# A transformer block in one kernel: wo's low parts on POOL around z, kv's masking behind the denominators, other PSUM banks for the kv transposes, and one more set of q logits

## The chip, the cores and the metric

The kernel runs on one core of a Trainium2 chip. The metric is the device time of the whole kernel in microseconds; lower is better. The core's engines are TensorE (PE, matmuls; PEld is its weight load), VectorE (DVE), ScalarE (ACT), GpSimd (POOL) and SyncE (SP), which issues most DMAs. Each works through its own queue in order and waits on semaphores for what others produce.

## The reference

Sequence 2048, width 512, 32 heads of 16, hidden size 1792 of the token MLP, all float32. The block is a linear attention with learned softmax features, then an MLP over the token axis:

```python
pq = einsum("bhsd,hdf->bhsf", q, w_phi); pk = einsum("bhsd,hdf->bhsf", k, w_phi)
phi_q = concat([softmax(pq), softmax(-pq)], -1)
phi_k = concat([softmax(pk), softmax(-pk)], -1)
kv  = einsum("bhsf,bhsd->bhfd", phi_k, v)
z   = einsum("bhsf->bhf", phi_k)
num = einsum("bhqf,bhfd->bhqd", phi_q, kv)
den = einsum("bhqf,bhf->bhq", phi_q, z)[..., None] + 1e-6
h   = x + (num / den merged over heads) @ wo          # q, k, v = layernorm(x) @ wqkv
u   = gelu(einsum("bsd,sf->bdf", layernorm(h), w1) + b1)
out = h + transpose(einsum("bdf,fs->bds", u, w2) + b2)
```

## The kernel before

The tokens are cut into 16 tiles of 128 (`NT`). Float32 products are made from high and low parts in fp32r: `mm3` (lines 59 to 63) issues hi*hi, lo*hi or hi*lo, and the third, so a 128x512 product over four blocks of the width is twelve matmuls. `split` (line 54) makes the parts: ACT copies the high part, another engine subtracts it.

**First stage** (from line 330). For each tile t: project and exponentiate k (`k_logits`), project v (`v_proj`), add to kv in PSUM (`kv`, line 188, tile `kvp`), normalise phi_k (`k_norm`) and add it to `zacc`, from which z comes. For six tiles q is projected here too: `q_mm` (line 304) projects the next tile of q into one of two PSUM banks of the pool `ps_q`; `q_logits` (line 309) takes the maxima and minima per head on DVE, writes the shifted logits to an `eq` tile on DVE (line 138) and, from the seventh tile on, a plain copy on ACT (line 140, the last reader of the bank). `negate` (line 149) finishes that half on POOL; `q_exp` is an exp on ACT; `q_sums` sums on DVE.

**Transition** (lines 352 to 453). From line 353 on the order of PE, DVE, ACT and POOL is the order in which the code issues, by hand; SP's order is left to the scheduler. Here the last tiles of v and kv are made, wo is loaded into `WO` (line 370) and split into `woh` (`wo_hi`, ACT) and `wol` (`wo_lo`, DVE). z is a product of `zacc` with ones (line 426), copied to `zB` on ACT. `s_ez` (line 374, POOL) multiplies an exponentiated q tile by z, `s_den` (line 378, six operations on DVE) makes from it the factor `W`, `s_pq` (line 393, POOL) multiplies the q tile by `W`. At its end kv is masked into `kvS` (DVE, line 449), transposed on PE into a bank of the pool `ps_v` (line 452) and copied to `kvB` on ACT (line 453). When the pools of the first stage close (line 456), the banks of `ps_k`, `ps_v` and `ps_kv` are used again by `ps_f` (MLP sums), `ps_t` (transposes and numerators, tiles `tn`) and `ps_o` (output products, tile `po`).

**Loop** (line 557, counter `it`, 19 passes). Per pass PE does `s_num(it-1)` (32 small matmuls with `kvB`, line 481), `s_wo(it-2)` (twelve matmuls with woh and wol into `po`), `s_tr(it)` (eight transposes into `tn`), one `q_mm` (two in it=1), and from it=4 on `fill` for the first MLP product. `lead` (line 396) issues `s_pq(it+1)`, `s_ez(it+3)`, a `negate`, the `q_mm` and a `q_exp`. DVE then does `s_ol` (the low part of the numerators, tile `ol`; its high part `oh` is ACT's), the logits, two sums and a denominator interleaved, then `s_h` (adds `po` to the loaded x as tile `h`, statistics), then the low parts of streamed weights (`wlo`). The one `tn` buffer is read by `oh` and `ol` before the next transposes, the one `po` buffer by `h` before the next `s_wo`. `FN[p]` and `FL[p]` count how far the fills and weight loads of F-pair p have come; the second pair starts (line 582) when all sixteen q logits are made.

After the loop come the rest of the first MLP product with its gelu (line 641) and the second product (line 689), both mostly PE.

Of the kernel before, what the change touches and what calls it, by code (L numbers as in the profile page):

```python
# [9 lines left out]
F32 = mybir.dt.float32  # L10
F32R = mybir.dt.float32r
AF = mybir.ActivationFunctionType
# [5 lines left out]
P = 128  # L18
S, D, H, DH, F = 2048, 512, 32, 16, 1792
NT = S // P  # L20
KD = D // P
# [12 lines left out]
def block_kernel(ctx: ExitStack, tc: tile.TileContext, x, xT, wT, phibd, wo, w1, b1, w2, b2,  # L34
                 kvmask, ident_in, out):
    nc = tc.nc
# [4 lines left out]
    ident = cst.tile([P, P], F32, name="ident")  # L41
# [28 lines left out]
    wqp = aq.enter_context(tc.tile_pool(name="wqp", bufs=1, side="right"))  # L70
    wqh = wqp.tile([P, KD, D], F32R, name="wqh")
    wql = wqp.tile([P, KD, D], F32R, name="wql")
    kvB = wqp.tile([P, 2, P], F32, name="kvB")
    wqp.tile([P, 504], F32, name="pad")
    wk = aq.enter_context(tc.tile_pool(name="wk", bufs=4, side="right"))

# [6 lines left out]
    wp = a1.enter_context(tc.tile_pool(name="wp", bufs=1))  # L83
# [1 line left out]
    wvh = wp.tile([P, KD, D], F32R, name="wvh")  # L85
    wvl = wp.tile([P, KD, D], F32R, name="wvl")
    zacc = wp.tile([P, NG, P], F32, name="zacc")
    kvS = wp.tile([P, 4, 64], F32, name="kvS")
    ps_k = a1.enter_context(tc.tile_pool(name="ps_k", bufs=2, space=PSUM))
    ps_v = a1.enter_context(tc.tile_pool(name="ps_v", bufs=2, space=PSUM))  # L90
    ps_kv = a1.enter_context(tc.tile_pool(name="ps_kv", bufs=1, space=PSUM))
# [26 lines left out]
    def proj(t, wh, wl, pool, name):  # L118
        o = pool.tile([P, D], F32, name=name, tag=name)
        for kt in range(KD):  # L120
            mm3(o, X[t][:, 0, kt, :], X[t][:, 1, kt, :], wh[:, kt, :], wl[:, kt, :],
                kt == 0, kt == KD - 1)
        return o
# [6 lines left out]
    def logit_ops(src, e, pool):  # L130

        v = src.rearrange("p (j h d) -> p j h d", h=2, d=DH)
        ev = signs(e)
        mx = wk.tile([P, NPR, 2], F32, name="mx")
        mn = wk.tile([P, NPR, 2], F32, name="mn")

        def shift():
            nc.vector.tensor_sub(ev[:, :, 0], v, mx.unsqueeze(3).to_broadcast([P, NPR, 2, DH]))
            if pool:
                nc.scalar.activation(ev[:, :, 1], v, AF.Copy)  # L140
                MN.append((ev, mn))
            else:
                nc.vector.tensor_sub(ev[:, :, 1], mn.unsqueeze(3).to_broadcast([P, NPR, 2, DH]), v)

        return [lambda: nc.vector.tensor_reduce(mx, v, axis=AX.X, op=ALU.max),
                lambda: nc.vector.tensor_reduce(mn, v, axis=AX.X, op=ALU.min),
                shift]
# [7 lines left out]
    def run(*lists):  # L155

        for i in range(max(map(len, lists))):
            for ops in lists:
                if i < len(ops):
                    ops[i]()  # L160

    def exps(t, e):
        nc.scalar.activation(e, e, AF.Exp, scale=r1[:, t:t + 1])

    def heads(e):
        return e.rearrange("p g (a d) -> p (g a) d", d=DH)
# [11 lines left out]
    def k_norm(t, z=True):  # L178
        sk = wk.tile([P, 2 * H], F32, name="sk", bufs=2)
        nc.vector.reduce_sum(sk, heads(PK[t]), axis=AX.X)  # L180
        nc.vector.reciprocal(sk, sk)
        nc.gpsimd.tensor_mul(heads(PK[t]), heads(PK[t]), sk.unsqueeze(2).to_broadcast([P, 2 * H, DH]))  # L182
        if z and t == 0:
            nc.gpsimd.tensor_copy(zacc, PK[t])
        elif z:
            nc.gpsimd.tensor_add(zacc, zacc, PK[t])  # L186

    def kv(t):

        for n in range(4):  # L190
            for c in range(4):
                g = n // 2 * 4 + c
                j = 2 * g + n % 2
                nc.tensor.matmul(kvp[32 * c:32 * c + 32, n, :], VS[t][:, 32 * j:32 * j + 32],
                                 PK[t][:, g, n % 2 * 64:n % 2 * 64 + 64], start=(t == 0 and n == 0),
                                 stop=(t == NT - 1), skip_group_check=True)
# [107 lines left out]
    def q_mm():  # L304
        if q["mm"] < NT:
            PS[q["mm"]] = proj(q["mm"], wqh, wql, ps_q, "pu")
            q["mm"] += 1

    def q_logits(lag):
        n = q["logits"]  # L310
        if n < min(NT, q["mm"] - lag + NT * (q["mm"] == NT)):
            EQ[n] = big.tile([P, NG, P], F32, name="eq", tag="big")
            q["logits"] += 1
            return logit_ops(PS[n], EQ[n], n >= len(Q_AT))
        return []

    def q_exp(lag):
        n = q["exp"]
        if n < min(NT, q["logits"] - len(MN) - lag):
            exps(n, EQ[n])  # L320
            q["exp"] += 1

    def q_sums(lag):
        n = q["sum"]
        if n < min(NT, q["exp"] - lag + NT * (q["exp"] == NT)):
            q["sum"] += 1
            return q_sum(n)
        return []
# [29 lines left out]
    woh = w2p.tile([P, KD, D], F32R, name="woh")  # L358
    wol = w2p.tile([P, KD, D], F32R, name="wol")

    def wo_hi(j):
        nc.scalar.activation(woh[:, j], WO[j], AF.Copy)

    def wo_lo(j):
        nc.vector.tensor_sub(wol[:, j], WO[j], woh[:, j])

    WO = {}
    for j in range(KD):
# [5 lines left out]
    def s_ez(t):  # L374
        EZ[t] = az.tile([P, NG, P], F32, name="ez")
        nc.gpsimd.tensor_mul(EZ[t], EQ[t], zB)  # L376
# [16 lines left out]
    def s_pq(t):  # L393
        nc.gpsimd.tensor_mul(heads(EQ[t]), heads(EQ[t]), W[t].rearrange("p g c h -> p (g c h)").unsqueeze(2).to_broadcast([P, 2 * H, DH]))  # L394

    def lead(it, mm):

        if 0 <= it + 1 < NT:
            s_pq(it + 1)
        if 0 <= it + 3 < NT:  # L400
            s_ez(it + 3)
        negate()
        for _ in range(mm):
            q_mm()
        q_exp(0)

    def v_kv():
        nonlocal v
        v_proj(v)
        kv(v - 1)  # L410
        v += 1
# [3 lines left out]
    nc.gpsimd.tensor_add(zacc, zacc, PK[NT - 2])  # L415
    q_mm()
    k_norm(NT - 1, False)
    v_kv()
    run(q_logits(0))
    nc.vector.tensor_add(zacc, zacc, PK[NT - 1])  # L420
    negate()
    q_exp(0)
    zB = big.tile([P, NG, P], F32, name="zB", tag="big")
    for g in range(2):
        pz = ps_k.tile([P, 4, P], F32, name="pk_ps")
        nc.tensor.matmul(pz, ones, zacc[:, 4 * g:4 * g + 4, :], start=True, stop=True)
        nc.scalar.activation(zB[:, 4 * g:4 * g + 4, :], pz, AF.Copy)  # L427
    s_ez(0)
    s_ez(1)
    q_mm()  # L430
    v_kv()
    run(s_den(0))
    run(q_logits(0))
    for j in range(KD):
        wo_hi(j)
    s_pq(0)
    negate()
    q_exp(0)
# [2 lines left out]
    v_kv()  # L441
    run(s_den(1))
    run(q_logits(0))
    for j in range(KD):
        wo_lo(j)
    assert v == NT
    kv(NT - 1)
    q_mm()
    nc.vector.tensor_mul(kvS, kvp, mask.unsqueeze(1).to_broadcast([P, 4, 64]))
    pt = ps_v.tile([P, 2, P], F32, name="pv")  # L450
    for b in range(2):
        nc.tensor.transpose(pt[:, b, :], kvS[:, 2 * b:2 * b + 2, :].rearrange("p n f -> p (n f)"), ident)
    nc.scalar.activation(kvB, pt, AF.Copy)


    a1.close()
# [6 lines left out]
    ps_o = a2.enter_context(tc.tile_pool(name="ps_o", bufs=1, space=PSUM, reuse_waits="tile"))  # L463
    HN, HT, PHT, OS, PO, VE = {}, {}, {}, {}, {}, {}

    def s_tr(t):
        PHT[t] = ak.tile([P, NG, P], F32, name="pht")
        ptr = ps_t.tile([P, 2, 4, P], F32, name="tn")
        for g in range(NG):
            nc.tensor.transpose(ptr[:, g // 4, g % 4, :], EQ[t][:, g, :], ident)  # L470
        for half in range(2):
            nc.scalar.activation(PHT[t][:, half * 4:half * 4 + 4, :], ptr[:, half], AF.Copy)  # L472

    def s_num(t):

# [12 lines left out]
    def s_ol(t):  # L488
        oh, ol, pn = OS[t]
        return [lambda: nc.vector.tensor_sub(ol, pn, oh)]  # L490
# [66 lines left out]
    for it in range(NT + 3):  # L557
        if 0 <= it < NT:
            s_x(it)
        if 0 <= it - 3 < NT:  # L560
            s_rstd(it - 3)
        if 0 <= it - 1 < NT:
            s_num(it - 1)
        if 0 <= it - 2 < NT:
            s_wo(it - 2)
        if it == 1:
            q_mm()
        if 0 <= it < NT:
            s_tr(it)
        lead(it, 1)  # L570
        den = s_den(it + 2) if it + 2 < NT else []
        run((s_ol(it - 1) if 0 <= it - 1 < NT else []) + q_logits(1) + (q_sums(0) if it > 0 else []), den)
        if it > 0:
            negate()
        if 0 <= it - 3 < NT:
            s_hn(it - 3)
        if 0 <= it - 2 < NT:
            s_h(it - 2)
        if FN[0] <= it - LAG:
            fill(0, ps_f)  # L580
        for _ in range(2):
            if q["logits"] == NT and FN[1] <= it - LAG:
                fill(1, ps_q)
        for p in range(2):
            if it >= LAG - 2 and FL[p] <= FN[p] + 1:
                fill_load(p)
# [198 lines left out]
```

## Time and profile before

| | |
|---|---|
| median of 3 runs | 568.13 us (567.6 to 568.39) |
| profiled execution | 566.03 us, of which 564.3 us span |
| mean granted PE clock | 0.986 |
| busy PE / PEld / DVE / ACT / POOL | 95% / 81% / 71% / 45% / 41% |
| longest groups on the chain that ended last | products into `py` (second MLP product) 25%, products into `pu` (q and first MLP product) 30% |

The page of the profile gives busy times per engine, the span in 40 slices, the DMA queues, the chain of work that ended last and the costliest groups of instructions. Other views give each engine's instructions in order of time with the idle time before them and what ended it, the waits of an engine summed by what it waited for, and the busy times in chosen stretches. In a row of the time view the first number is the start in us from the span's start, the second the duration (of several where "xN" stands), then engine, line, operation, and tiles written and read; in brackets the engine's idle time before it and its releaser. A row of a stretch gives its length, then the busy time of PE, PEld, DVE, ACT and POOL with counts, the granted clock, the DMA share and GB/s.

### The profile page before, as it was taken

Reading aid. Unit: us, or ns where it says so; the run is one execution under the profiler, and the core shown is the slowest. Engines: PE = TensorE matmul, PEld = TensorE weight load, DVE = VectorE, ACT = ScalarE, POOL = GpSimd, SP = SyncE. Lnnn points to the kernel's source line nnn. Section 1 sums busy time; section 2 is a strip of 40 time slices with the busy share of each in tenths; the row PEclk is TensorE's granted clock in tenths of the full one; section 3 lists DMA queues with packets and bytes.
Section 4 is the critical chain, followed back from the end, with each engine's and each line's share of the span. In section 5 each row is a group of like instructions: output and inputs, shape, how many; then the busy total and the mean of one; then the engine's idle time right before and its main releaser. Section 6 shows DMA issues by size and latency. Waiting matters only on the chain.

```text
span 564.3 us, 9893 instructions
## 1 busy us (share of the span) xinstructions
PE 535.8 (95%) x3872; PEld 456.4 (81%) x3872; DVE 401.3 (71%) x730; ACT 256.7 (45%) x402; POOL 229.4 (41%) x179
## 2 busy tenths in 40 slices
PE   7999999999778888999999999999999999999996
PEld 6787778777556666877778778888889999999996
DVE  4884999974975659999644893222765888878874
ACT  5599834423343336444454752332643333333330
POOL 1369799785834766889643220000000111101110
PEclk9999999999988979999999999999999999999999
DMA  8444301022200212333325544333102664456631
GB/s 290 129 113 131 113 20 57 1 58 95 75 1 20 76 56 53 117 113 114 123 88 175 153 143 127 105 98 93 57 20 74 150 150 105 131 140 150 150 68 45
DMA packets 52014, 56.06 MB, mean 99 GB/s; under 512 B 3840, under 2 KB 41600, under 8 KB 51968
## 3 DMA queue, kind: packets, MB, share of 16 engines
q1 hardware_dynamic: 49808, 51.64, 29.8%
q0 software_dynamic: 2016, 3.67, 4.7%
q8 instruction: 30, 0.49, 0.4%
q14 instruction: 16, 0.13, 0.1%
q10 hardware_dynamic: 144, 0.13, 0.1%
HBM read 47.04 MB, written 8.39 MB: 98 GB/s over the span
## 4 chain that ended last, share of the span: by engine, by line
PE 84%; DVE 6%; ACT 4%; DMA 2%; issue 1%; POOL 1%; SPq 0%; DVEq 0%; POOLq 0%; ACTq 0%
PE py L678 25%; PE pu L61 10%; PE pu L63 10%; PE pu L62 10%; PE po L61 3%; PE pk_ps L61 3%; PE pk_ps L62 3%; PE pk_ps L63 3%; PE tn L470 3%; PE po L62 2%; PE po L63 2%; PE pv L61 2%; PE pv L62 2%; PE pv L63 2%; PE tn L481 2%
## 5 line engine op out<-in xcount | busy, mean ns | idle before, releaser
L57 DVE TENSOR_TENSOR wlo<-wraw,whi 128x512 fp32r<-128x512 f32 (+1 forms) x84 | 99.8, 1199 | 69.5 <-ACT whi L56 69.3
L56 ACT ACTIVATE whi<-wraw 128x512 fp32r<-128x512 f32 (+1 forms) x84 | 81.9, 985 | 128.1 <-PE py L678 73.8
L678 PE MATMUL py<-uf,whi 128*128 128x256 f32 x560 | 96.2, 283 | 0.0
L716 POOL DMA_DIRECT2D out<-ot x14 | 12.5, 999 | 205.0 <-DVE ot L714 205.0
L61 PE MATMUL pu<-hs,whi 128*128 128x512 f32 x224 | 87.8, 395 | 0.6 <-ACT eq L140 0.6
L62 PE MATMUL pu<-hs,whi 128*128 128x512 f32 x224 | 87.4, 390 | 0.0
L63 PE MATMUL pu<-hs,wlo 128*128 128x512 f32 x224 | 86.3, 391 | 0.4 <-DVE wlo L57 0.4
L678 PEld LDWEIGHTS py<-uf,whi 128*128 128x128 f32 x560 | 83.3, 192 | 0.0
L678 PE MATMUL py<-uf,wlo 128*128 128x256 f32 x280 | 69.9, 283 | 0.0
L63 PEld LDWEIGHTS pu<-hs,wlo 128*128 128x128 f32 x224 | 42.0, 188 | 10.2 <-DVE wlo L57 1.5
L61 PEld LDWEIGHTS pu<-hs,whi 128*128 128x128 f32 x224 | 42.2, 189 | 9.4 <-ACT eq L140 1.1
L678 PEld LDWEIGHTS py<-uf,wlo 128*128 128x128 f32 x280 | 49.7, 192 | 0.0
L62 PEld LDWEIGHTS pu<-hs,whi 128*128 128x128 f32 x224 | 42.2, 189 | 8.5
L472 ACT ACTIVATE pht<-tn 128x512 f32<-128x512 f32 x32 | 17.4, 596 | 49.0 <-PE tn L470 49.0
L376 POOL TENSOR_TENSOR ez<-eq,zB 128x1024 f32<-128x1024 f32 x16 | 38.6, 2418 | 2.2 <-ACT zB L427 2.2
L61 PE MATMUL pu<-wqh,xs 128*128 128x512 f32 x64 | 28.8, 450 | 10.9 <-ACT eq L140 10.9
L678 PE MATMUL py<-un,whi 128*128 128x256 f32 x224 | 38.4, 283 | 0.0
L182 POOL TENSOR_TENSOR pk<-pk,sk 128x1024 f32<-128x1024 f32 x16 | 31.1, 1942 | 9.3 <-ACT xs L56 3.0
L394 POOL TENSOR_TENSOR eq<-eq,w 128x1024 f32<-128x1024 f32 x16 | 31.0, 1938 | 6.1 <-DVE w L391 6.1
L678 PEld LDWEIGHTS py<-un,whi 128*128 128x128 f32 x224 | 33.2, 192 | 0.1
L186 POOL TENSOR_TENSOR zacc<-zacc,pk 128x1024 f32<-128x1024 f32 x13 | 31.2, 2403 | 0.5
L57 POOL TENSOR_TENSOR xs<-xraw,xs 128x512 fp32r<-128x512 f32 x16 | 20.4, 1292 | 25.1 <-ACT xs L56 25.1
(152 smaller groups left out, 1161.0 us busy)
## 6 DMA issues: line engine op xcount, KB each, us to landing
wraw<-in_w SPq DMA_DIRECT2D x112, 256.0 KB, 2.9
xraw<-in_xT SPq DMA_DIRECT2D x16, 256.0 KB, 3.2
xh<-in_x SPq DMA_DIRECT2D x16, 256.0 KB, 2.6
h<-in_x SPq DMA_DIRECT2D x16, 256.0 KB, 2.9
out<-h SPq DMA_DIRECT2D x16, 256.0 KB, 2.5
out<-ot POOLq DMA_DIRECT2D x14, 256.0 KB, 4.3
wraw<-in_wT SPq DMA_DIRECT2D x12, 256.0 KB, 5.3
wo<-in_wo SPq DMA_DIRECT2D x4, 256.0 KB, 4.1
```

What stands on the lines that cost most here:

```text
L56: nc.scalar.activation(hi, src, AF.Copy)
L57: lo_engine.tensor_sub(lo, src, hi)
L61: nc.tensor.matmul(o, ah, bh, start=first, stop=False)
L62: nc.tensor.matmul(o, ah, bl, start=False, stop=False)
L63: nc.tensor.matmul(o, al, bh, start=False, stop=last)
L182: nc.gpsimd.tensor_mul(heads(PK[t]), heads(PK[t]), sk.unsqueeze(2).to_broadcast([P, 2 * H, DH]))
L186: nc.gpsimd.tensor_add(zacc, zacc, PK[t])
L376: nc.gpsimd.tensor_mul(EZ[t], EQ[t], zB)
L394: nc.gpsimd.tensor_mul(heads(EQ[t]), heads(EQ[t]), W[t].rearrange("p g c h -> p (g c h)").unsqueeze(2).to_broadcast([P, 2 * H, DH]))
L470: nc.tensor.transpose(ptr[:, g // 4, g % 4, :], EQ[t][:, g, :], ident)
L472: nc.scalar.activation(PHT[t][:, half * 4:half * 4 + 4, :], ptr[:, half], AF.Copy)
L678: nc.tensor.matmul(o, a[x], b[:, y], start=start and i == 0, stop=stop and i == 2, skip_group_check=True)
```

## The change

The edit touches the transition and the first pass of the loop.

- `wo_lo` subtracts on POOL instead of DVE. All four `wo_hi` and the first two `wo_lo` are issued after `k_norm` of the last tile; the other two `wo_lo` after the first two `s_ez`.
- The first `q_exp` of the transition is issued after z's copies instead of before them.
- The last `q_mm` of the transition is issued ahead of `kv(NT - 1)` instead of behind it.
- `kvS` moves to another pool; its mask stays behind the second denominator and logits, no longer behind the four `wo_lo`. Its transposes and the copy to `kvB` become `s_kv`, issued in it=0 after `s_tr(0)`, with a PSUM tile of `ps_o` instead of `ps_v`.
- In it=0 one more `q_logits` is issued, so that eleven sets of logits are made by its end instead of ten.

```diff
@@ wqp (stays to the loop's end) / wp (first stage only)
     kvB = wqp.tile([P, 2, P], F32, name="kvB")
+    kvS = wqp.tile([P, 4, 64], F32, name="kvS")
...
-    kvS = wp.tile([P, 4, 64], F32, name="kvS")
...
     def wo_lo(j):
-        nc.vector.tensor_sub(wol[:, j], WO[j], woh[:, j])
+        nc.gpsimd.tensor_sub(wol[:, j], WO[j], woh[:, j])
...
     k_norm(NT - 1, False)
+    for j in range(KD):
+        wo_hi(j)
+    wo_lo(0)
+    wo_lo(1)
     v_kv()
     run(q_logits(0))
     nc.vector.tensor_add(zacc, zacc, PK[NT - 1])
     negate()
-    q_exp(0)
     zB = big.tile([P, NG, P], F32, name="zB", tag="big")
...
         nc.scalar.activation(zB[:, 4 * g:4 * g + 4, :], pz, AF.Copy)
+    q_exp(0)
     s_ez(0)
     s_ez(1)
+    wo_lo(2)
+    wo_lo(3)
     q_mm()
     v_kv()
     run(s_den(0))
     run(q_logits(0))
-    for j in range(KD):
-        wo_hi(j)
     s_pq(0)
...
     run(q_logits(0))
-    for j in range(KD):
-        wo_lo(j)
     assert v == NT
+    q_mm()
     kv(NT - 1)
-    q_mm()
     nc.vector.tensor_mul(kvS, kvp, mask.unsqueeze(1).to_broadcast([P, 4, 64]))
-    pt = ps_v.tile([P, 2, P], F32, name="pv")
-    for b in range(2):
-        nc.tensor.transpose(pt[:, b, :], kvS[:, 2 * b:2 * b + 2, :].rearrange("p n f -> p (n f)"), ident)
-    nc.scalar.activation(kvB, pt, AF.Copy)
...
+    def s_kv():
+
+        pt = ps_o.tile([P, 2, P], F32, name="po")
+        for b in range(2):
+            nc.tensor.transpose(pt[:, b, :], kvS[:, 2 * b:2 * b + 2, :].rearrange("p n f -> p (n f)"), ident)
+        nc.scalar.activation(kvB, pt, AF.Copy)
...
         if 0 <= it < NT:
             s_tr(it)
+        if it == 0:
+            s_kv()
         lead(it, 1)
         den = s_den(it + 2) if it + 2 < NT else []
         run((s_ol(it - 1) if 0 <= it - 1 < NT else []) + q_logits(1) + (q_sums(0) if it > 0 else []), den)
+        if it == 0:
+            run(q_logits(0))
```

## The prediction, made before the changed kernel was run

> **What bounds the kernel now.** I read the page first, then the list of waits on PE, then each engine's instructions in order of time around the edited lines, then the busy time by stage. `q_mm` n, `kv` n, logits n below are those of token tile n; `it` is the loop's counter.
>
> ```profile
> span 564.3 us, 9893 instructions
> PE 535.8 (95%) x3872; PEld 456.4 (81%) x3872; DVE 401.3 (71%) x730; ACT 256.7 (45%) x402; POOL 229.4 (41%) x179
> PE pu L61 <- ACT eq L140: 11.6, 5, 2.8
> PE po L61 <- DVE h L505: 1.2, 1, 1.2
> ```
>
> PE is busy 95% of the span. These two rows of its waits (us, times, longest) and three single ones quoted below, 5.4 us together, are most of what a named producer makes it wait; all lie between 148 and 223 us, just where the edit is. The stages show what that costs twice over (PE, PEld, DVE, ACT, POOL busy, then granted clock):
>
> ```profile
> 148.64:162.05 13.41, 9.16 (x67) 7.07 (x67) 11.21 (x14) 3.46 (x6) 7.73 (x5) 0.87 0.23 76
> 162.05:173.78 11.73, 9.03 (x65) 6.85 (x64) 5.59 (x12) 3.21 (x5) 7.86 (x5) 0.85 0.00 0
> 194.18:208.53 14.35, 11.65 (x72) 8.92 (x71) 8.64 (x18) 5.06 (x8) 11.41 (x10) 0.76 0.24 77
> 225.11:291.20 66.09, 66.09 (x607) 52.35 (x614) 54.52 (x117) 32.60 (x56) 49.65 (x42) 1.00 0.37 120
> ```
>
> Where PE idles, its clock then falls too (0.87, 0.85, 0.76). From 225 us on PE is busy for all of 66.09 us, so a microsecond saved before that point reaches the end.
>
> **Change, part 1: from the last `kv` to the first loop products.**
>
> ```profile
> 148.64 0.65 PE L194 MATMUL kvp<-pk,vs 128*32 128x64 f32 x32 [1.12 <-ACT vs L176]
> L365 DVE TENSOR_TENSOR wol<-wo,woh x4: 678/1931/2861, 148.4 to 154.9; 128x512 fp32r<-128x512 f32 x4
> 155.50 0.41 DVE L449 TENSOR_TENSOR kvS<-kvp,mask 128x256 f32<-128x256 f32 x1
> 155.96 0.44 PE L452 MATMUL pv<-ident,kvS 128*128 128x128 f32 x2 [3.68 <-DVE kvS L449]
> 156.96 1.94 PE L470 MATMUL tn<-ident,eq 128*128 128x128 f32 x8 [0.56 <-ACT kvB L453]
> 158.56 0.78 PE L61 MATMUL pu<-wqh,xs 128*128 128x512 f32 x1
> 162.05 0.67 PE L481 MATMUL tn<-pht,kvB 64*32 64x128 f32 x32
> ```
>
> Three waits stand in a row. `kv` 15 waits 1.12 for its value tile; the change puts `q_mm` 9 (2.9 us of PE) ahead of it. `kvS` stands behind four subtractions on DVE (678 to 2861 ns, median 1931, from 148.4 on); they leave for POOL, so it can run right after `kv` 15. The kvS transposes had the value projections' banks, which the first eight transposes want next, hence 0.56; they move to the output product's bank, and behind those eight, whose 0.79 us cover the `kvS` mask (0.41). Gone: 1.12 + 3.68 + 0.56 = 5.36.
>
> What the moved work costs where it lands:
>
> ```profile
> 122.74 2.02 SPq L370 DMA_DIRECT2D wo<-in_wo  x4
> wo<-in_wo SPq DMA_DIRECT2D x4, 256.0 KB, 4.1
> 144.70 2.18 ACT L362 ACTIVATE woh<-wo 128x512 fp32r<-128x512 f32 x4
> 132.81 0.69 ACT L176 ACTIVATE vs<-pv,r 128x512 f32<-128x512 f32 x1 [5.08 <-PE pv L63]
> 131.83 1.22 DVE L420 TENSOR_TENSOR zacc<-zacc,pk 128x1024 f32<-128x1024 f32 x1
> 134.06 1.05 POOL L153 TENSOR_TENSOR eq<-mn,eq 128x512 f32<-128x512 f32 x1 [2.90 <-ACT eq L140]
> L57 POOL TENSOR_TENSOR xs<-xraw,xs 128x512 fp32r<-128x512 f32 x16 | 20.4, 1292 | 25.1 <-ACT xs L56 25.1
> 133.23 1.98 PE L426 MATMUL pk_ps<-zacc,ones 128*128 128x512 f32 x4
> 136.21 1.06 ACT L427 ACTIVATE zB<-pk_ps 128x512 f32<-128x512 f32 x2
> 137.35 4.73 POOL L376 TENSOR_TENSOR ez<-eq,zB 128x1024 f32<-128x1024 f32 x2 [2.23 <-ACT zB L427]
> 152.91 1.50 POOL L153 TENSOR_TENSOR eq<-mn,eq 128x512 f32<-128x512 f32 x1
> ```
>
> The `wo` loads have landed by about 129 (124.76 + 4.1). The four `wo_hi` (2.18) fit into ACT's 5.08 idle before 132.81: nothing. The first two `wo_lo` at 1.29 (the same operation on POOL) would fill POOL's 2.90 idle before 134.06. But DVE's `zacc` add, which the z products on PE wait for, then runs beside them. Both read two SBUF tiles, and the row of `wol`, which ran beside POOL, shows what such a meeting does: 0.68 for the shortest of four, 2.86 for the longest; POOL's negation at 152.91 took 1.50 there against 1.05. Bounds: 0 if DVE wins, 1.3 if it waits one whole `wo_lo`. I take 0.5: POOL starts at 131.2 (134.06 - 2.90), DVE arrives at 131.83 and waits to about 132.45; the z products start at 133.7, not at 133.2. The second `wo_lo` is then behind the add, so the negation starts 0.9 late.
>
> The Trainium skill, "SBUF — State Buffer", section "Who interferes with whom", says that a VectorE instruction with two SBUF inputs and a GpSimd one that reads SBUF take turns at a shared port, the later blocked for the whole of the earlier. That rule speaks against this edit; by it the stall is what is left of the `wo_lo`, some 0.6, and the row agrees in kind.
>
> z's copies on ACT no longer stand behind an exp: products to 133.7 + 1.98 = 135.7, the second copy (half of 1.06) to 136.3, so `ez` starts 1.0 earlier than 137.35. The last two `wo_lo` (2.6) follow the two `ez` (4.73): `s_pq(0)` starts at 143.7, and it, a negation, two `ez`, another `s_pq` and the negation of set 8 take POOL to about 154.4, as before (152.91 + 1.50), since they are no longer stretched. Behind that negation stands exp 8 on ACT, then the logits' copies. s_tr(0) needs what `s_pq(0)` writes by 151.5, and has it by 145.7: a cover of 6 us; beyond it PE would wait.
>
> So: z 0.5 late; `q_mm` 9 at 148.64 - 1.12 + 0.5 = 148.0, `kv` 15 at 150.9, first transposes at 151.5, those of kvS (0.44) at 152.3, `q_mm` 10 at 152.65 (158.56 before), first `tn<-pht,kvB` at 155.6 (162.05).
>
> **Part 2: the loop.**
>
> ```profile
> 169.25 0.50 PE L61 MATMUL pu<-wqh,xs 128*128 128x512 f32 x1 [2.70 <-ACT eq L140]
> 173.78 0.67 PE L481 MATMUL tn<-pht,kvB 64*32 64x128 f32 x32
> 181.03 0.50 PE L61 MATMUL pu<-wqh,xs 128*128 128x512 f32 x1 [2.76 <-ACT eq L140]
> 183.98 0.67 PE L481 MATMUL tn<-pht,kvB 64*32 64x128 f32 x32
> 191.23 0.50 PE L61 MATMUL pu<-wqh,xs 128*128 128x512 f32 x1 [2.76 <-ACT eq L140]
> 201.36 0.80 PE L61 MATMUL pu<-wqh,xs 128*128 128x512 f32 x1 [2.70 <-ACT eq L140]
> 208.53 0.67 PE L481 MATMUL tn<-pht,kvB 64*32 64x128 f32 x32
> 212.00 1.03 PE L470 MATMUL tn<-ident,eq 128*128 128x128 f32 x8
> 212.79 0.48 PE L61 MATMUL pu<-hs,whi 128*128 128x512 f32 x1
> 214.34 0.67 PE L481 MATMUL tn<-pht,kvB 64*32 64x128 f32 x32
> ```
>
> `q_mm` n needs the bank of `q_mm` n-2, free once logits n-2 are read. Today logits 10 come in it=1 after `q_mm` 12 in PE's order: a wait in each of it=1 to 4, 2.70 + 2.76 + 2.76 + 2.70 = 10.92. With one more set in it=0 logits 10 to 13 are read an iteration before they are wanted. All four go.
>
> The clock: first transposes 158.56 - 156.96 = 1.60 against 0.79 (212.00 to 212.79); `q_mm` 10 3.49 against 2.95 (181.03 to 183.98); `q_mm` 12 4.53 against 2.95; `q_mm` 15 with six products after it 7.17 against 2.95 + 1.55 (212.79 to 214.34). Together 0.81 + 0.54 + 1.58 + 2.67 = 5.60, gone if the new waits, none above 1.3, leave the clock alone.
>
> The Trainium skill, "TensorE: Matmul & The Clock Gate", Part 1, has the clock halved after an idle window of about 3.4 us that runs free of the program. Here waits of 2.70 were followed by slow matmuls and waits of 2.76 were not; by the page's figure all 5.60 return.
>
> What is late next is DVE:
>
> ```profile
> 159.73 0.22 DVE L391 TENSOR_TENSOR w<-smq,den 128x64 f32<-128x64 f32 x1
> 175.19 0.69 DVE L490 TENSOR_TENSOR ol<-tn,oh 128x512 fp32r<-128x512 f32 x1 [6.10 <-ACT oh L485]
> 180.80 0.69 DVE L505 TENSOR_TENSOR h<-po,h 128x512 f32<-128x512 f32 x1
> 182.60 1.28 DVE L57 TENSOR_TENSOR wlo<-wraw,whi 128x512 fp32r<-128x512 f32 x2
> ```
>
> An iteration of DVE is 5.61 (`ol` to `h`) + 1.80 (`h` to `wlo`) + 0 to 1.28 (more beside POOL), so 7.4 to 8.7; PE's, without its wait, is 183.98 - 173.78 - 2.76 = 7.44. In it=0 the extra set adds three passes of the size of `ol` to DVE, some 1.9, and puts a copy ahead of `oh` 0 on ACT. Chained from `kvS` at 151.6 to 152.0: logits 9 and denominators to 156.0 (4.0, as from 155.91 to 159.95), logits 10 to 157.9, their copy to 158.5, `oh` 0 to 159.1, `ol` 0 to 159.8; PE is ready for s_tr(1) at 159.05: a wait of 0.8. `ol` 1 at 165.0 costs nothing; it=2 has 5.61 + 1.80 + two `wlo`, of which one meets POOL (2.1 in all), so `ol` 2 runs from 174.5 to 175.2; PE, with `s_wo` 1 from 171.4 to 174.3, waits 0.9 for it before s_tr(3); `h` 1 ends at 174.5 + 5.61 + 0.69 = 180.8, and `s_wo` 2, ready at 179.5, waits 1.3. Bounds for these three: 0 if DVE keeps up, about 7 if every DVE iteration takes 9. After it=5 logits are done and DVE has slack (54.52 of 66.09). The fills that begin an iteration earlier move 2.7 us of PE work, no sum; the 1.21 on `h` becomes a similar one on `ol`: nothing.
>
> **Sum**: 5.36 + 10.92 + 5.60 = 21.88 gone; 0.5 + 0.8 + 0.9 + 1.3 = 3.5 new; net 18.4. The profiled execution took 566.03 (span 564.30 and 1.73 around it): 547.6. The median shown, 568.13, is 2.10 above that execution, so I predict **549.7**. `kvS` in another pool moves addresses only: nothing, bounded by the 0.8 either way that the three runs differ (567.6 to 568.39).
>
> **Rivals.**
> A, DVE keeps up: no new wait, 1.21 falls too: 568.1 - 23.1 = 545.0. For it: DVE idles 6.10 before `ol` today. Against: that idle is PE's own waiting. Chance 0.15.
> B, DVE is the bound in it=2 to 5: at 9.0 a piece new waits take 4 x (9.0 - 7.44) + 0.8 = 7.0, not 3.0: gain 14.4, 553.7. For it: the `wol` row. 0.14.
> C, the extra set does not do what it says, since logits come late again and the four waits return with their clock: only 5.36 + 0.81 + 0.54 - 0.5 = 6.2 is left, 561.9. Against: chained above, the copy of set 10 is done at 158.5, `q_mm` 12 wants it at 160.7. 0.06.
> D, slower: POOL becomes the loop's bound. It is busy 7.86 in the stage of 162.05 to 173.78, above PE's 7.44 already, and meets DVE's `wlo`. From 8.9 an iteration over the 13 that follow it=3 it eats the gain; at 9.0 it costs (9.0 - 7.44) x 13 = 20.3: 570.0. Against: it is busy 49.65 of 66.09 later, and what it makes is wanted an iteration on. 0.04.
>
> **How the numbers follow.** The forecast has 0.61, with its own range 547 to 552.5. To leave out no more than 0.2 the range takes A's end and B: 545.0 to 557.5. A change within 0.2% (1.1 us) cannot be told from none here. Faster 0.94 (forecast, A, B, C and a remainder), same 0.02, slower 0.04.
>
> **What would show it.** Right: no PE wait on `eq` above 0.7, none on `kvS` or `kvB`; granted clock 1.00 in all stages from 123 us; first `tn<-pht,kvB` near 155.6, the fifth near 189 (208.53 before); a `zacc` add above 1.22; new PE waits on `ol` and `h` of about 1 each. Wrong: waits on `eq` that stay (C); long waits on `ol` or `h` (B); a slow clock after a short wait, which would keep up to 5.6; the z products later than 134.5.

## The result, and the profile after

| | median | executions | against the kernel before beside it |
|---|---|---|---|
| changed kernel | 545.12 us | 544.33 to 547.04 (4) | before 567.87; ratio 0.9609 [0.9577, 0.9640] |
| changed kernel, measured again later | 545.16 us | 544.74 to 547.11 (6) | before 563.80; ratio 0.9666 [0.9639, 0.9693] |
| its profiled execution | 544.96 us, span 543.2 | granted clock 0.997 | before 566.03, span 564.3, clock 0.986 |

It is faster by 22.8 us in the first comparison and by 18.6 us in the second (differences of the medians; a ratio here is one of means); the forecast was 18.4. The changed kernel gives the same time in both; the kernel before does not, and how far that can be explained is told below. The list of waits on PE, of the changed kernel (us, times, longest):

```profile
PE tn L468 <- DVE ol L495: 1.3, 2, 0.8
PE pu L63 <- DVE wlo L57: 1.1, 3, 0.6
PE po L61 <- DVE h L510: 1.0, 1, 1.0
PE pu L61 <- ACT eq L140: 0.6, 1, 0.6
PE pk_ps L429 <- DVE zacc L424: 0.3, 1, 0.3
```

Waits on `eq` fell from 11.6 to 0.6; those on `kvS`, `kvB` and `vs` are gone. New are two on `ol`, one on `zacc` and two more on `wlo`; the one wait on `h` now stands in it=4 (1.00) instead of it=6 (1.21). Of the forecast waits, those on `zacc`, on `ol` before s_tr(1) and on `h` came; the one before s_tr(3) did not, and the second on `ol` (0.52) stands before s_tr(7). In order of time (of eight transposes, kvS transposes, first numerators, then the waits that are left in the loop's first passes):

```profile
149.88 0.65 PE L194 MATMUL kvp<-pk,vs 128*32 128x64 f32 x32
150.47 1.09 PE L468 MATMUL tn<-ident,eq 128*128 128x128 f32 x8
151.40 0.38 PE L476 MATMUL po<-ident,kvS 128*128 128x128 f32 x2
154.49 0.67 PE L486 MATMUL tn<-pht,kvB 64*32 64x128 f32 x32
158.92 1.06 PE L468 MATMUL tn<-ident,eq 128*128 128x128 f32 x8 [0.83 <-DVE ol L495]
162.67 0.67 PE L486 MATMUL tn<-pht,kvB 64*32 64x128 f32 x32
179.03 0.50 PE L61 MATMUL po<-woh,oh 128*128 128x512 f32 x1 [1.00 <-DVE h L510]
186.96 0.67 PE L486 MATMUL tn<-pht,kvB 64*32 64x128 f32 x32
194.14 0.50 PE L61 MATMUL pu<-hs,whi 128*128 128x512 f32 x1 [0.64 <-ACT eq L140]
```

Last `kv`, transposes and the first products of the loop follow one another without a gap. The fifth `tn<-pht,kvB` stands at 186.96 (208.53 before). By stage (length; busy PE, PEld, DVE, ACT, POOL; granted clock; DMA share, GB/s; the first row begins within `q_mm` 9, not at `kv` 15):

```profile
147.94:154.49 6.55, 6.55 (x64) 5.03 (x62) 3.82 (x9) 2.65 (x5) 5.23 (x3) 1.00 0.66 197
154.49:162.67 8.18, 7.35 (x66) 5.58 (x65) 6.93 (x15) 4.05 (x7) 6.31 (x4) 1.00 0.00 0
169.82:177.36 7.54, 7.46 (x65) 5.58 (x64) 7.44 (x17) 4.18 (x9) 6.50 (x5) 1.00 0.31 104
177.36:186.96 9.60, 8.60 (x72) 6.79 (x71) 9.39 (x22) 5.78 (x11) 8.40 (x7) 1.00 0.17 56
204.00:272.00 68.00, 67.48 (x610) 53.07 (x589) 53.92 (x119) 35.19 (x60) 51.44 (x44) 1.00 0.35 112
```

The clock is 1.00 where it was 0.87, 0.85 and 0.76. DVE is busy for 7.44 of 7.54 and 9.39 of 9.60 us. In it=4 it, not PE (8.60), sets the pace; in it=3 PE is busy nearly throughout as well (7.46), and DVE costs it at most some 0.4, since the pass ahead of it took 7.15 (162.67 to 169.82). The meeting of `zacc` and `wo_lo` that was priced at 0.5 (DVE, then POOL):

```profile
130.95 1.65 DVE L424 TENSOR_TENSOR zacc<-zacc,pk 128x1024 f32<-128x1024 f32 x1
130.24 3.49 POOL L365 TENSOR_TENSOR wol<-wo,woh 128x512 fp32r<-128x512 f32 x2
132.75 1.96 PE L429 MATMUL pk_ps<-zacc,ones 128*128 128x512 f32 x4 [0.33 <-DVE zacc L424]
140.13 2.53 POOL L365 TENSOR_TENSOR wol<-wo,woh 128x512 fp32r<-128x512 f32 x2
```

The add takes 1.65, not 1.22; the first pair of `wo_lo` takes 3.49, the second, which on DVE meets no longer operation on two SBUF tiles than one of 0.22, 2.53; PE loses 0.33.

### The profile page after: what moved, and what is told of

It is laid out like the page before. It is cut to its first block, busy times and chain, and to the rows that moved or that the text cites. A ratio compares the mean times of both kernels' runs of the same rounds, so it can differ in the third digit from the quotient of the medians.

```text
span 543.2 us, 9896 instructions
## 1 busy us (share of the span) xinstructions
PE 528.6 (97%) x3872; PEld 449.7 (83%) x3872; DVE 393.8 (73%) x726; ACT 256.5 (47%) x402; POOL 234.2 (43%) x183
## 4 chain that ended last, share of the span: by engine, by line
PE 87%; DVE 7%; ACT 3%; DMA 2%; issue 1%; SPq 0%; DVEq 0%; ACTq 0%
PE py L687 25%; PE pu L61 11%; PE pu L63 11%; PE pu L62 10%; PE pk_ps L61 3%; PE pk_ps L62 3%; PE pk_ps L63 3%; PE po L61 3%; PE pv L61 3%; PE pv L62 3%; PE pv L63 3%; PE po L62 2%; PE po L63 2%; PE tn L468 2%; PE kvp L194 2%; PE tn L486 1%
## 5 line engine op out<-in xcount | busy, mean ns | idle before, releaser
L57 POOL TENSOR_TENSOR hs<-hn,hs 128x512 fp32r<-128x512 f32 x16 | 20.6, 1289 | 21.2 <-ACT hs L56 21.2
```

The lines of the kernel that those rows point to most:

```text
L57: lo_engine.tensor_sub(lo, src, hi)
```

## The experiments

Besides medians I use one interval of the profiled executions, since it leaves out how the first loads landed: from the end of `kv` 12 (before, PE starts the z products there, at 133.23) to the sixteenth `tn<-pht,kvB`. Each figure is of one execution. It is 157.63 in the kernel before (133.23 to 290.86) and 136.27 in the changed one (132.42 to 268.69; 136.36 in its second profile).

**Part 2 taken out.** The changed kernel without the extra set:

```diff
-        if it == 0:
-            run(q_logits(0))
```

> The changed kernel without the one more set of q logits in it=0; all else as changed. The prediction's theory: the four waits of q_mm 12 to 15 on the copy of the logits come back (2.6 to 2.8 each, 10.9 together) with the slow clock behind some of them (up to 4.3), the new waits on ol and h (about 2.4) go: 10 to 14 us longer than the changed kernel, about 557. Rival, that the transition alone carries the gain and the waits were hidden anyway: within 2 us of the changed kernel. First tn<-pht,kvB unchanged near 154.5 to 155.5 in either.

Measured: 557.94 us (556.99 to 558.87), ratio to before 0.9892 [0.9861, 0.9923]; interval 151.08. Its waits on PE:

```profile
PE pu L61 <- ACT eq L140: 12.1, 5, 3.2
PE po L61 <- DVE h L510: 1.2, 1, 1.2
```

The four waits are back, the waits on `ol` are gone, and slow matmuls follow two of the four (three of them are shown; the fourth is 2.70):

```profile
162.48 0.80 PE L61 MATMUL pu<-wqh,xs 128*128 128x512 f32 x1 [3.24 <-ACT eq L140]
175.29 0.80 PE L61 MATMUL pu<-wqh,xs 128*128 128x512 f32 x1 [2.76 <-ACT eq L140]
186.99 0.50 PE L61 MATMUL pu<-wqh,xs 128*128 128x512 f32 x1 [2.76 <-ACT eq L140]
```

The set is worth 12.8 us by the medians (14.8 by the interval, whose execution was the longest of the four); that the transition alone carries the gain falls.

**Part 2 alone.** The kernel before with only those two lines added.

> The kernel before with only the one more set of q logits in it=0. The prediction's theory: the two halves add up; the waits of q_mm 12 to 15 go, the three of the transition (1.1, 3.7, 0.6) stay with the slow first transposes: about 11 to 13 us shorter than before, 555 to 557. Rival: without the transition's edits DVE is late by the four wo_lo, so the set only moves the waits to ol and h: 562 or more, with waits on ol and h of 2 to 4 each in it=1 to 4.

Measured: 551.74 us (551.34 to 554.54), 0.9793 [0.9759, 0.9827], beside a kernel before of 564.01; interval 142.79.

```profile
PE pv L452 <- DVE kvS L449: 3.7, 1, 3.7
PE kvp L194 <- ACT vs L176: 1.1, 1, 1.1
PE po L61 <- DVE h L505: 1.0, 1, 1.0
PE tn L470 <- DVE ol L490: 1.0, 2, 0.5
PE pu L61 <- ACT eq L140: 0.6, 1, 0.6
```

The waits of the transition stand, those on `eq` are gone, and the new ones are as small as in the changed kernel. In the interval the halves add up: 14.84 (157.63 - 142.79) from the set and 6.55 (157.63 - 151.08) from the rest make 21.39, and the change has 21.36. That they agree to 0.03 is partly luck, since the slow clock differs by more than that from one execution to the next.

**kvS in the other pool, alone.**

```diff
+    kvS = wqp.tile([P, 4, 64], F32, name="kvS")
...
-    kvS = wp.tile([P, 4, 64], F32, name="kvS")
```

> The kernel before with only kvS in the other pool. The prediction put this at nothing: within 0.15% of before. Rival, to explain that the changed kernel came out some 4 us faster than forecast: the shifted addresses speed up loads or matmuls somewhere; then 1 us or more shorter, with stages before 122 us that are shorter than before's.

Measured: 565.34 us (561.84 to 568.50, 12 executions) against 564.01 (561.78 to 568.26, 17): ratio 1.0013 [0.9983, 1.0043]. No difference shown; the addresses are not where the surplus came from. The spread of both, some 6.5 us, became the clue: the granted clock of these executions runs from 0.982 to 0.997, and the longest have a low clock (568.26 at 0.985, 561.78 at 0.997 and at 0.992).

**The changed kernel again, beside more executions of before.**

> The changed kernel itself, once more and beside more runs of the kernel before, because that kernel's runs spread from 561.8 to 568.3 in the first job with granted clocks from 0.982 to 0.997. If the gain over forecast (22.8 against 18.4) came from executions of before that met more slow clock than usual, the two medians stand 18 to 20 us apart here, and the changed kernel's own runs spread less (clock 0.995 to 0.998). Rival: the change is worth 22 us or more against any execution; then 22 or more here too.

Measured: 545.16 (544.74 to 547.11, clock 0.994 to 0.999) against 563.80 (562.01 to 566.08, clock 0.988 to 0.994): 18.6 us, ratio 0.9666. The first comparison's executions of before had taken 566.32 to 568.39; these are 4 us shorter, and the changed kernel is not. The rival, 22 or more against any execution, falls. Three of the first comparison's four executions of before are those of the table before, taken ahead of the changed kernel; beside the fourth (566.32) the gain is 21.2.

**wo_lo back on DVE, late.**

```diff
-        nc.gpsimd.tensor_sub(wol[:, j], WO[j], woh[:, j])
+        nc.vector.tensor_sub(wol[:, j], WO[j], woh[:, j])
...
     run(s_den(1))
     run(q_logits(0))
+    for j in range(KD):
+        wo_lo(j)
     assert v == NT
```

(The four calls at their new places are taken out.)

> The changed kernel with the four wo_lo back on DVE, behind the second denominator and set 8, ahead of the kvS mask. Theory: they run beside POOL from about 146.5 and take some 7 us, so the mask ends near 153.5, the kvS transposes wait some 2 us behind the first eight, and logits 9 are 3 us late, which q_mm 11 and the copy to oh 0 feel: 3 to 5 us longer than the changed kernel. Rival, that the mask's place behind the eight transposes and q_mm 9 hides them: under 1 us.

Measured: 548.44 us (546.95 to 549.70); interval 139.79, 3.5 longer than the changed kernel's. DVE, then PE:

```profile
146.58 7.20 DVE L365 TENSOR_TENSOR wol<-wo,woh 128x512 fp32r<-128x512 f32 x4
153.70 0.41 DVE L449 TENSOR_TENSOR kvS<-kvp,mask 128x256 f32<-128x256 f32 x1
154.17 0.69 PE L474 MATMUL po<-ident,kvS 128*128 128x128 f32 x2 [2.50 <-DVE kvS L449]
```

The wait of 2.50 is as priced; from the kvS transposes to the first `tn<-pht,kvB` it then takes 4.67 (to 158.84), 3.09 in the changed kernel: slow matmuls behind the wait. So four `wo_lo` in DVE's queue ahead of the mask cost 3.5. This is the price of their place and not of the engine: further below they are on DVE in an earlier place, and the kernel is no slower for it.

**Two more edits of the transition, undone one at a time (one profile each).** First the place and the bank of the kvS transposes:

```diff
     nc.vector.tensor_mul(kvS, kvp, mask.unsqueeze(1).to_broadcast([P, 4, 64]))
+    pt = ps_v.tile([P, 2, P], F32, name="pv")
+    for b in range(2):
+        nc.tensor.transpose(pt[:, b, :], kvS[:, 2 * b:2 * b + 2, :].rearrange("p n f -> p (n f)"), ident)
+    nc.scalar.activation(kvB, pt, AF.Copy)
...
-        if it == 0:
-            s_kv()
```

> The changed kernel with the kvS transposes and the copy to kvB back in the transition, in the value projections' banks, ahead of the first eight transposes. Theory: PE waits for the mask after kv 15 (about 0.5 to 0.7) and then for the copy to kvB (about 0.56) before s_tr(0): the first tn<-pht,kvB comes 1.1 to 1.3 later, counted from the end of kv 12, and the gap stays to the end. Rival: only the bank wait of 0.56 comes back, since the mask was short enough either way.

```profile
151.39 0.44 PE L454 MATMUL pv<-ident,kvS 128*128 128x128 f32 x2 [0.55 <-DVE kvS L451]
152.40 1.06 PE L472 MATMUL tn<-ident,eq 128*128 128x128 f32 x8 [0.56 <-ACT kvB L455]
```

Both waits come back. The first `tn<-pht,kvB` comes 1.35 later (23.42 from `kv` 12's end, 22.07 in the changed kernel), the interval is 1.0 longer (137.28): 0.35 is given back where the changed kernel waits for `ol` anyway. Then the order of `kv` 15 and `q_mm` 9:

```diff
-    q_mm()
     kv(NT - 1)
+    q_mm()
```

> The changed kernel with kv 15 ahead of q_mm 9 again. Theory: kv 15 waits for vs 15, which on ACT stands behind exp 7 and a negation on POOL, near 147.3 where kv 14 ends at 146.9: 0.4 to 0.5 lost, not the 1.12 of before, since z and so POOL's chain are earlier; against it the mask is ready before s_tr(0) as it is already, nothing back. Rival: nothing lost, the wait had gone with the earlier chain; or all of 1.1.

```profile
147.13 0.65 PE L194 MATMUL kvp<-pk,vs 128*32 128x64 f32 x32 [0.45 <-ACT vs L176]
```

0.45 comes back, not 1.12; first `tn<-pht,kvB` 0.38 later, interval 136.49, 0.2 longer. This edit is worth little. That most of the 1.12 had gone with the earlier chain on POOL and ACT is likely, but not shown: no run moves the first `q_exp` back ahead of z's copies. Singly these undone edits give 3.5, 1.0 and 0.2 of the transition's 6.55; the rest is not assigned.

**What limits the changed kernel now.** Three edits at the new waits. One: the extra set's copy on ACT goes behind `oh` 0 (the argument is handed on by `q_logits`).

```diff
-                nc.scalar.activation(ev[:, :, 1], v, AF.Copy)
-                MN.append((ev, mn))
+                def copy():
+                    nc.scalar.activation(ev[:, :, 1], v, AF.Copy)
+                    MN.append((ev, mn))
+                LATE.append(copy) if late else copy()
...
             s_num(it - 1)
+            while LATE:
+                LATE.pop()()
...
-            run(q_logits(0))
+            run(q_logits(0, True))
```

> The changed kernel, but the extra set's copy on ACT is issued behind oh 0 in it=1, not in it=0. Theory: the wait of 0.83 before s_tr(1) was the copy ahead of oh 0 on ACT's queue plus the extra set on DVE; oh 0 then runs near 155.3, ol 0 right behind the extra set near 156.9, and s_tr(1) waits 0; the copy still precedes q_mm 12. 0.8 us shorter up to the second tn<-pht,kvB. Rival: DVE sets it, ol 0 stays near 158 and the wait stays; or the gained 0.8 is given back at the next ol or h, since DVE is the bound in it=2 to 4 (total gain under 0.3).

Measured: 544.33 us (543.47 to 545.25), interval 135.28, 1.0 shorter; the wait of 0.83 before s_tr(1) is gone and not given back. Two: all four `wo_lo` on DVE right behind the `zacc` add.

```diff
-        nc.gpsimd.tensor_sub(wol[:, j], WO[j], woh[:, j])
+        nc.vector.tensor_sub(wol[:, j], WO[j], woh[:, j])
...
-    wo_lo(0)
-    wo_lo(1)
...
     nc.vector.tensor_add(zacc, zacc, PK[NT - 1])
+    for j in range(KD):
+        wo_lo(j)
...
-    wo_lo(2)
-    wo_lo(3)
```

> The changed kernel with all four wo_lo on DVE right behind its zacc add, in DVE's 5.25 us of idle time there, none on POOL. Theory: the add no longer meets a wo_lo (1.22 again, not 1.65), the z products wait 0 instead of 0.33, and the s_pq, ez and negations of the transition come 1 to 2.5 us earlier on POOL, which nothing on PE waits for: 0.3 us shorter, within noise of the changed kernel. Rival: POOL's chain did matter; more than 1 us shorter.

```profile
131.03 1.22 DVE L422 TENSOR_TENSOR zacc<-zacc,pk 128x1024 f32<-128x1024 f32 x1
132.16 3.35 DVE L365 TENSOR_TENSOR wol<-wo,woh 128x512 fp32r<-128x512 f32 x4
137.81 1.22 DVE L385 TENSOR_REDUCE tz<-ez 128x64 f32<-128x1024 f32 x1 [2.30 <-POOL ez L376]
```

Measured: 544.12 us (542.93 to 545.95), interval 135.92, 0.35 shorter. The add is back at 1.22, four `wo_lo` take 3.35 with one POOL instruction beside them, not 7.20, and DVE still idles 2.30. So POOL is not needed for `wo_lo`: what the change won with it, it won by taking them out from ahead of the mask. Both edits together:

> Both edits, the copy of the extra set behind oh 0 and the four wo_lo early on DVE. Theory: the sum of the two, about 1 us shorter than the changed kernel if the 0.8 is not given back to DVE, else 0.3.

Measured: 543.49 us (542.67 to 543.89), interval 134.89: the sum, 1.4. Three: on top of both, the first two weight tiles' low parts, 1.28 us of DVE in it=2, go to POOL (the engine is handed on to `split`).

```diff
-                fill_load(p)
+                fill_load(p, nc.gpsimd if it == LAG - 2 else nc.vector)
```

> As the one with both edits (oh 0 ahead, wo_lo early on DVE), and the low parts of the two weight tiles loaded in it=2 are made on POOL, not on DVE. Theory: DVE is the bound in it=2 to 4 by just these 1.28 us; without them h 1 comes 1.2 earlier and the wait of 1.0 before s_wo 2 is gone, the fifth tn<-pht,kvB 1.0 earlier, some 542.5 in all. Rival: POOL, with 2.6 us more in it=2, delays rstd and the negation of set 13, the wait on eq of 0.6 before the first fill of the second pair grows, and nothing is won.

Measured: 542.35 us (541.29 to 543.15); interval 133.65, 1.24 shorter again. The wait on `h` is gone, the one on `eq` stays at 0.6:

```profile
PE pu L63 <- DVE wlo L57: 1.0, 2, 0.7
PE pu L61 <- ACT eq L143: 0.6, 1, 0.6
PE tn L470 <- DVE ol L497: 0.5, 1, 0.5
```

This version is the fastest here: 0.9610 of before [0.9571, 0.9649], 2.8 us under the changed kernel's median. That these 1.28 us on DVE held up the passes it=3 and it=4 is shown (7.16 and 8.68 instead of 7.45 and 9.58 with both edits); that POOL would suffer is not so.

## Why the prediction was right, and where its sum was off

Both mechanisms held, the waits taken out of the transition and the four waits on the copied logits, but the time fell into the stated range only just: 545.12 lies outside the forecast's own 547 to 552.5 and 0.1 above the end that rival A had set. That the range reached so far is luck, for A's mechanism did not come true.

**Part 1.** Shown. The three waits went. First `tn<-pht,kvB`: 22.07 after the end of `kv` 12, against 28.82 before, 6.75 gained where the sum had 5.36 + 0.81 + 0.54 - 0.5 = 6.2. The z stall was 0.33, not 0.5. The cover named for `kv` 15 was larger than thought needed: undone alone, the swap costs 0.45, not 1.12. The bank and place of the transposes are worth 1.0, getting `wo_lo` out from ahead of the mask 3.5.

**The port.** The `zacc` add ran 1.65 instead of 1.22, and at 1.22 with no `wo_lo` on POOL. The Trainium skill's rule on the shared port ("SBUF — State Buffer", "Who interferes with whom") agrees: the first `wo_lo`, 1.28 from 130.24, would end at 131.5, and an add of some 1.2 begun there ends at 132.7; it ended at 132.60.

**Part 2.** Shown by taking the set out and by adding it alone. From the first to the fifth `tn<-pht,kvB` the kernel before took 46.48 (162.05 to 208.53), the changed one 32.47 (154.49 to 186.96): 14.0 gained, 12.2 forecast (10.92 + 1.58 + 2.67 - 3.0). Of the three new waits two came as priced (0.83 for 0.8, 1.00 for 1.3); the 0.9 before s_tr(3) did not, since neither `wlo` of it=2 met POOL: the two took 1.28, not 2.1. The 1.8 of difference can be followed from the lengths of the passes. A pass without a wait takes 7.15, and 8.68 with six more products (both in the version with the first `wlo` on POOL). The four passes of the changed kernel took 8.18, 7.15, 7.54 and 9.60, 2.3 more than these, where 3.0 was forecast: 0.7. The other 1.2 lies in what the rows leave out: the two passes of before with a wait of 2.76 and no slow matmul took 10.20, that is 3.05 more than 7.15 and not 2.76. The idle time of a row counts from the end of the last matmul, and PE can start the next some 0.24 before that (transposes begun at 212.00 end at 213.03, and the next matmul begins at 212.79), so each of the four waits cost about 0.29 more than its row says. For the same reason the 7.44 that the prediction gave a pass of PE was too long.

**After it=4.** "The 1.21 on `h` becomes a similar one on `ol`" was too dear: 0.52, and 0.6 gained to the ninth `tn<-pht,kvB`. From there to the sixteenth the two are equal (50.07 each). Behind it 1.1 was lost (273.44 before, 274.51 after); waits on `wlo` of 1.1 instead of 0.4 are part of it. The second profile of the changed kernel has 0.4 and 273.38 there, so this varies between executions.

**The profiled pair.** 0.8 from before the edit (133.23 against 132.42; first loads landed sooner), 6.75, 14.0, 0.6, less 1.1: 21.1, the difference of the spans, 564.3 - 543.2.

**What missed.** The forecast of 549.7 was 4.6 too long, in two parts. The sum was 2.7 short (18.4 for the 21.1 of the profiled pair), as shown above. And the forecast carried the 2.10 between the median before, 568.13, and the profiled execution over to the changed kernel, where only 0.2 of it is found (545.12 against 544.96). The prediction sized the slow clock at 5.60 from one execution, as if it were a property of the kernel; in the kernel before it differs from one execution to the next (0.982 to 0.997 of clock, 561.7 to 568.4 us), and with its waits the changed kernel loses most of that spread (0.994 to 0.999, 544.3 to 547.1). Against the later executions of before the change is worth 18.6. That this is so near to 18.4 is luck too: the sum was too small, and the median of these executions is 2.2 shorter than the profiled one from which the sum was taken.

Not explained is why the first executions of before were all long: of the 38 taken later only four reach 566.32, the shortest of those four. Their clock is not on record, so that slow clock made them long is likely, not shown.

**Rivals.** A (no new wait on DVE) falls as a mechanism, since 2.7 us of waits came, though its 545.0 is the time measured; B falls, DVE's passes took 7.3 to 8.7, not 9; C falls with the `eq` row; D falls: POOL was busy 51.44 of 68.00 us later, and 2.6 us more on it in it=2 cost nothing.

## What to carry to other kernels

Where two buffers turn between a producer and its reader, see in the hand-written order whether the reader of set n stands behind the producer of set n+2: one set issued ahead, once, takes the wait out of every pass, and then look which engine is next (here DVE, by under 1.3 us a pass). Price a moved subtraction by what runs beside it where it lands: the same four took 7.2 us beside POOL's work and 3.35 some 14 us earlier, beside one instruction of POOL. And before a gain in slow clock is booked, look how the clock differs between executions of the same kernel.

## What the runs showed of the hardware that was not expected

The same waits slow the clock in one execution and not in the next. In the kernel before, waits of 2.70, 2.76, 2.76 and 2.70 were followed by slow matmuls after the first and the last. In the variant with only kvS moved, whose waits are the same, it was after the first and the second:

```profile
169.52 0.50 PE L61 MATMUL pu<-wqh,xs 128*128 128x512 f32 x1 [2.70 <-ACT eq L140]
181.33 0.80 PE L61 MATMUL pu<-wqh,xs 128*128 128x512 f32 x1 [2.76 <-ACT eq L140]
192.93 0.50 PE L61 MATMUL pu<-wqh,xs 128*128 128x512 f32 x1 [2.76 <-ACT eq L140]
```

Its passes from one `tn<-pht,kvB` to the next took 11.70, 11.60, 10.24 and 11.50 where the kernel before took 11.73, 10.20, 10.20 and 14.35 (the fourth has six more products, 1.5). Against 7.15, and 8.68 with those products, a wait of 2.7 so costs between 0.1 and 3.0 beyond its row; waits of 1.0 or less were followed by no slow matmul that these profiles show.

The traces hold more on when it happens. In each profile the granted clock is 0.50 or 1.00, and its changes lie whole multiples of 3.41 us apart. These are stretches between such points in the kernel before (length, then PE's busy time; the clock is third from the end). The first and the fifth hold most of a wait of 2.70 and are followed by a slow stretch, the second and the last row; the third and the fourth hold most of a wait of 2.76 and are followed by stretches at 1.00:

```profile
166.54:169.96 3.42, 0.72 (x4) 0.63 (x4) 2.51 (x8) 2.61 (x4) 0.69 (x1) 1.00 0.00 0
169.96:173.37 3.41, 3.41 (x10) 2.65 (x9) 0.00 (x0) 0.00 (x0) 3.41 (x3) 0.50 0.00 0
176.78:180.20 3.42, 1.50 (x11) 1.12 (x9) 3.42 (x10) 1.83 (x3) 0.00 (x0) 1.00 0.00 0
187.02:190.44 3.42, 1.45 (x11) 1.08 (x9) 3.42 (x10) 1.87 (x3) 1.19 (x1) 1.00 0.00 0
197.26:200.68 3.42, 1.40 (x11) 1.03 (x9) 3.42 (x10) 1.98 (x3) 1.65 (x1) 1.00 0.00 0
200.68:204.09 3.41, 2.73 (x7) 2.17 (x8) 3.05 (x8) 2.48 (x5) 2.40 (x3) 0.50 0.24 69
```

From 118 us on to the last products, in all thirteen profiles of this case, the ten such stretches at full clock with PE busy for 1.40 us or less were each followed by one at 0.50, and none with 1.45 or more was. So in these profiles it is not the length of a wait that decides, but how much work falls into the same stretch, and where the stretches lie differs from one execution to the next. This is a regularity of these profiles; no run was made to test it. The Trainium skill, "TensorE: Matmul & The Clock Gate", Part 1, has a window of about 3.4 us that runs free of the program: the stretches of 3.41 us agree with that; that one with PE busy for as much as 1.40 us is followed by a slow one does not follow from its figure alone.
